# Chunk attention before a squared-ReLU FFN: the first 512 tokens in two halves of the heads, loaded in 1 KB packets

## The chip, the cores and the metric

The kernel runs on one core of a Trainium2 chip. The metric is the device time of one execution in microseconds (us), as the median of several runs. The engines are TensorE (PE, with its weight loads shown apart as PEld), VectorE (DVE), ScalarE (ACT), GpSimd (POOL) and SyncE (SP), which here only issues DMAs.

## What is computed

```python
scores = scale * np.matmul(q_c, k_c.transpose(0, 1, 2, 4, 3))   # chunks of 64 tokens, D = 64
scores = scores - np.max(scores, axis=-1, keepdims=True)
attn = np.exp(scores)
attn = attn / (np.sum(attn, axis=-1, keepdims=True) + 1e-09)
out = np.matmul(attn, v_c)
...
x = np.ascontiguousarray(attn_out.transpose(0, 2, 1, 3)).reshape(B * S, H * D)
h = np.maximum(x @ w_in, 0.0)
return (h * h @ w_out).astype(np.float32)
```

q, k and v are (8, 8, 576, 64): 8 batches, 8 heads, 576 tokens in 9 chunks of 64, 64 numbers a head, all float32. After attention inside each chunk, the 4608 tokens with 512 numbers each go through w_in (512 x 2048), a squared ReLU and w_out (2048 x 512).

## The kernel before

**Tiling.** The tokens are cut into 18 groups of 256 (four chunks each) and the groups into nine blocks of 512. A group's attention makes `x` (token on the partition); its transpose, `xT`, feeds the FFN of the block. `ffn_in` (L359) multiplies by w_in and squares: for each of 16 slices of 128 columns four matmuls (L366), a ReLU on ScalarE (L377) and a square on VectorE (L381) or ScalarE (L379). The second product of block 0 is `ffn_out_by_ft` (L517, matmuls L524), of the later blocks `ffn_out` (L399, matmuls L434), which needs sums of quarters of w_out (`w_sum`, L76) from VectorE.

**Order of the work.** The order is written out by hand. Each engine takes its instructions in the order in which the program names them and waits at semaphores; TensorE too. From L557 to L581 stands the prelude: loads of groups 0 and 1, then their attention, mixed with calls of `keep_busy` (L233), which are matmuls of the identity with itself whose result nobody reads. After it, the loads of the weights are named (L583 to L592), and the loop over blocks (L594) puts the attention of coming groups into numbered slots between the FFN's pieces.

**Loads.** SP issues all loads of one list, one after another: for groups 0 and 1 q, k, q, k (`qk_pieces`, L99: two neighbouring tokens on a partition, all 8 heads, so 512 bytes contiguous in DRAM), then V (`v_pieces`, L145: one token on a partition, 256 bytes contiguous; even heads into `ve_sb`, odd heads into `vo_sb`, the odd ones shifted by 64 partitions, nine DMAs for the two groups), then w_in tile 0, and after it seven more of w_in (`load_w_in`, L159, 1 KB contiguous) and eight of w_out (`load_w_out`, L168). Both weights go through five buffers `w_st` and are cast to bf16 by POOL (L165, L173). A load that finds eight others of the queue unfinished waits for the eighth before it. q and k have five buffers each.

**Attention of a group in the prelude.** `transpose_qk` (L201, as `TE`): 16 transposes on TensorE for q and 16 for k (L190; the high half of each float32 is taken as bf16), copied out of PSUM by VectorE (q) and ScalarE (k), L199. `scores` (L257, as `SC`): 32 matmuls of 64x64 (L276), exp on ScalarE (L287). `values` (L289, as `AV`): for each 128 tokens 16 matmuls (L303) with V, whose extra column of ones gives the sum, then reciprocal (L310) and multiplication (L311) on VectorE. `transpose_x_early` (L218): four transposes (L225) and a copy to `xT` (L230). The FFN of block 0 (`first_ffn_in`, L555) takes its first two slices for tokens 0 to 255, then for tokens 256 to 511, and then the rest for all 512.

**PSUM.** `ps_ffn` has four banks, used in turn by FFN, fillers and these transposes; `ps_att` two double banks.

Of the kernel before, what the change touches and what calls it, by code (L numbers as in the profile page):

```python
# [10 lines left out]
FP32 = mybir.dt.float32  # L11
BF16 = mybir.dt.bfloat16
AF = mybir.ActivationFunctionType
ALU = mybir.AluOpType
# [3 lines left out]
def kernel(  # L18
# [9 lines left out]
    nc = tc.nc  # L28

    B, H, S, D = q.shape  # L30
# [3 lines left out]
    scale = 1.0 / float(D) ** 0.5  # L34
    n_hp = H // 2
    n_dt = d_model // 128
# [4 lines left out]
    blocks = [[g, g + 1] for g in range(0, n_grp, 2)]  # L41
# [6 lines left out]
    chunks = whole[:-2] + rest + whole[-2:]  # L48
# [7 lines left out]
    BT = GT * max(len(b) for b in blocks)  # L56

    const_pool = ctx.enter_context(tc.tile_pool(name="const", bufs=1))
    w_pool = ctx.enter_context(tc.tile_pool(name="w", bufs=1))
    wst_pool = ctx.enter_context(tc.tile_pool(name="wst", bufs=5))  # L60
    in_pool = ctx.enter_context(tc.tile_pool(name="qk", bufs=5))
    att_pool = ctx.enter_context(tc.tile_pool(name="att", bufs=3))
    ffn_pool = ctx.enter_context(tc.tile_pool(name="ffn", bufs=1))
    ps_ffn = ctx.enter_context(tc.tile_pool(name="ps_ffn", bufs=4, space=bass.MemoryType.PSUM))
    ps_att = ctx.enter_context(tc.tile_pool(name="ps_att", bufs=2, space=bass.MemoryType.PSUM))
# [5 lines left out]
    ident = const_pool.tile([128, 128], BF16, name="ident")  # L71
# [4 lines left out]
    w_sum = w_pool.tile([128, 3, n_ft // 2, d_model // 2], BF16, name="w_sum")  # L76
# [22 lines left out]
    def qk_pieces(g):  # L99
        q_sb = in_pool.tile([128, 2, H, D], FP32, name="q_sb")  # L100
        k_sb = in_pool.tile([128, 2, H, D], FP32, name="k_sb")
        qk[g] = (q_sb, k_sb)

        def pairs(dst, src, p, m, b, s):
            return lambda: nc.sync.dma_start(
                out=dst.rearrange("p t h d -> p (t h d)")[p:p + m // 2, :].rearrange(
                    "p (h e) -> p h e", h=H),
                in_=src[b, :, s:s + m, :].rearrange("h (s i) d -> s h (i d)", i=2))

        if is_whole(g):  # L110
            yield pairs(q_sb, q, 0, GT, *chunks[g][0])
        else:
            for c in range(4):
                yield pairs(q_sb, q, c * CH // 2, CH, *chunks[g][c])
        if g < FIRST_DMA_T:
            yield pairs(k_sb, k, 0, GT, *chunks[g][0])
            return
        for t, p, m, b, s in runs(g):
            yield lambda t=t, p=p, m=m, b=b, s=s: nc.sync.dma_start(
                out=k_sb[p:p + m, t, :, :],  # L120
                in_=k[b, :, s:s + m, :].rearrange("h s d -> s h d"))
# [5 lines left out]
    for g in range(n_grp):  # L127
        if is_whole(g):
# [3 lines left out]
            b, s = chunks[g][0]  # L132
# [12 lines left out]
    def v_pieces(g):  # L145
        for t, p, m, b, s in runs(g):
            yield lambda t=t, p=p, m=m, b=b, s=s: nc.sync.dma_start(
                out=v_even[g % NV][p:p + m, t, :, 0:D],
                in_=v[b, 0::2, s:s + m, :].rearrange("h s d -> s h d"))
        for n, p, m, b, s in odd_loads[g]:  # L150
            yield lambda n=n, p=p, m=m, b=b, s=s: nc.sync.dma_start(
                out=v_odd[n % NO][p:p + m, :, 0:D],
                in_=v[b, 1::2, s:s + m, :].rearrange("h s d -> s h d"))

    def go(pieces):
        for f in pieces:
            f()

    def load_w_in(i, n_cast=1):  # L159
        cols = slice(i * 256, (i + 1) * 256)  # L160
        st = wst_pool.tile([128, 1024], FP32, name="w_st").rearrange("p (a f) -> p a f", a=n_dt)
        nc.sync.dma_start(out=st, in_=moe_w_in[:, cols].rearrange("(a p) f -> p a f", p=128))
        n = 256 // n_cast
        for c in range(0, 256, n):
            nc.gpsimd.tensor_copy(  # L165
                out=w_in_bf[:, :, i * 256 + c:i * 256 + c + n], in_=st[:, :, c:c + n])
# [8 lines left out]
    xTs = {}  # L175
    place = {}
# [3 lines left out]
    state = {}  # L180
# [20 lines left out]
    def transpose_qk(g, q_pool, k_pool):  # L201
        if ("qkT", g) not in state:
            state["qkT", g] = att_pool.tile(
                [128, 2, 2, n_hp, 128], BF16, name="qkT", bufs=4)
        qkT = state["qkT", g]
        for which, pool in enumerate((q_pool, k_pool)):
            if pool is None:
                continue
            copy = nc.scalar.copy if which else nc.vector.tensor_copy
            if pool is ps_ffn:  # L210
                bank = pool.tile([128, 512], FP32, name="ps_ffn")
            else:
                bank = pool.tile([128, 1024], FP32, name="ps_att")
            bank = bank.bitcast(BF16)[:, 0:1024]
            transpose_paired(g, which, bank)
            copy_paired(copy, qkT[:, which], bank)

    def transpose_x_early(g, t):  # L218
        j, c = place[g]
        if j not in xTs:  # L220
            xTs[j] = att_pool.tile([128, BT // 128, n_dt, 128], BF16, name="xT", bufs=2)
        psb = ps_ffn.tile([128, 512], FP32, name="ps_ffn").bitcast(BF16)
        x = state["x", g]
        for hp in range(n_hp):
            nc.tensor.transpose(  # L225
                out=psb[:, hp * 128:(hp + 1) * 128],
                in_=x[:, t, hp].rearrange("p a d -> p (a d)"),
                identity=ident)
        copy = nc.vector.tensor_copy if t else nc.scalar.copy
        copy(  # L230
            out=xTs[j][:, c // 128 + t].rearrange("p h q -> p (h q)"), in_=psb[:, 0:512])

    def keep_busy(n):  # L233
        ps = ps_ffn.tile([128, 512], FP32, name="ps_ffn")
        for _ in range(n):
            nc.tensor.matmul(out=ps[:, 0:128], lhsT=ident, rhs=ident, start=True, stop=True)
# [101 lines left out]
    SC, AV, XT = scores, values, transpose_x  # L338
# [4 lines left out]
    def TE(g):  # L343
        transpose_qk(g, ps_ffn, ps_ffn)
# [3 lines left out]

    def TK(g):
        transpose_qk(g, None, ps_ffn)  # L350

    def XE(g):
        for t in range(2):
            transpose_x_early(g, t)

    gTs = {}
    FT_ORDER = [*range(n_ft // 2, n_ft), *range(n_ft // 2)]
# [189 lines left out]
    def pieces(grps):  # L547
        for g in grps:
            yield from qk_pieces(g)
        for g in grps:  # L550
            yield from v_pieces(g)
# [2 lines left out]
    HT = BT // 2  # L554
    first_ffn_in = ffn_in(0, [(0, HT, (0, 1)), (HT, HT, (0, 1)), (0, BT, range(2, n_ft))])  # L555

    go(pieces([0, 1]))  # L557
    load_w_in(0, n_cast=2)
    TE(0)
    keep_busy(8)  # L560
    SC(0)
    keep_busy(6)
    TE(1)
    keep_busy(8)
    SC(1)
    keep_busy(10)
    AV(0, [0])
    keep_busy(4)
    AV(0, [1])
    keep_busy(8)  # L570
    transpose_x_early(0, 0)
    keep_busy(10)
    transpose_x_early(0, 1)
    AV(1, [0])
    keep_busy(8)
    AV(1, [1])
    transpose_x_early(1, 0)
    next(first_ffn_in)
    transpose_x_early(1, 1)
    next(first_ffn_in)  # L580
    keep_busy(4)  # L581

    for i in range(1, 8):  # L583
        load_w_in(i)
# [101 lines left out]
```

## Time and profile before

| what | value |
|---|---|
| runs | 290.56, 291.59, 297.44 us; median 291.59 us |
| profiled execution | span 286.0 us from first to last instruction; its own time is not shown beyond that |
| TensorE busy | 270.7 us, 95% of the span |
| VectorE, ScalarE, GpSimd busy | 187.9, 161.6, 56.5 us |
| DMA | 141841 packets, 57.10 MB |

The profile is one execution recorded by the hardware. Its page gives busy times, a line of 40 equal slices of the span for each engine (a digit is the busy share in tenths), and groups of instructions by line. The timeline lists, in order of time, start, duration, engine, line, operation, output and inputs, and how often; in brackets how long the engine sat idle before it and what released it. The list of waits gives for each engine and line what it waited for: total, times, longest. The DMA view gives packets, bytes and rate in a stretch of time.

### The profile page before, as it was taken

How to read it: one execution, taken by the hardware profiler on the slowest of the kernel's cores; microseconds unless marked ns; L12 is line 12 of the kernel's file. 1: busy time of each engine (PE TensorE's matmuls, PEld its weight loads, DVE VectorE, ACT ScalarE, POOL GpSimd, SP SyncE). 2: the span in 40 equal slices, each digit the busy share in tenths (PEclk: the TensorE clock that was granted, in tenths of full speed). 3: DMA queues.
4: the chain of work that ended last, by engine and by line, in shares of the span. 5: the costliest groups of instructions: out<-in, count | busy, mean ns of one | idle time of the engine just before them, and what ended most of it. 6: DMA issues, size and time to landing. Idle time of an engine off the chain costs nothing. (4 is left out here: it accounts for less than half of the span.)

```text
span 286.0 us, 7260 instructions
## 1 busy us (share of the span) xinstructions
PE 270.7 (95%) x2999; PEld 179.5 (63%) x3002; DVE 187.9 (66%) x307; ACT 161.6 (57%) x272; POOL 56.5 (20%) x89
## 2 busy tenths in 40 slices
PE   1989998999999999999979999999999999999994
PEld 1864444788784488448834784488448844884583
DVE  1274514889872497479637973896479648955792
ACT  1537704687437853885377638763876387318710
POOL 2035933244063002100300021002100300050012
PEclk9999999999999999999999999999999999999999
DMA  7999999999999999999999999399898941232003
GB/s 199 240 320 331 314 330 238 306 215 182 248 233 265 232 223 208 278 252 175 246 224 237 178 201 286 70 154 223 222 254 181 193 154 39 40 92 55 2 18 130
DMA packets 141841, 57.10 MB, mean 200 GB/s; under 512 B 110640, under 2 KB 137520, under 8 KB 141808
## 3 DMA queue, kind: packets, MB, share of 16 engines
q1 hardware_dynamic: 138768, 47.33, 77.1%
q0 software_dynamic: 2896, 9.18, 10.0%
q8 instruction: 23, 0.38, 0.6%
q10 hardware_dynamic: 144, 0.13, 0.1%
q14 instruction: 10, 0.08, 0.1%
HBM read 36.70 MB, written 9.44 MB: 161 GB/s over the span
## 5 line engine op out<-in xcount | busy, mean ns | idle before, releaser
L366 PE MATMUL ps_ffn<-xT,w_in_bf 128*128 128x512 bf16 (+1 forms) x648 | 130.5, 356 | 1.1 <-DVE xT L230 0.7
L381 DVE TENSOR_TENSOR gT<-rl 128x512 bf16<-128x512 f32 (+2 forms) x134 | 75.3, 590 | 63.8 <-ACT rl L377 62.5
L377 ACT ACTIVATE rl<-ps_ffn 128x512 f32<-128x512 f32 (+2 forms) x162 | 86.2, 549 | 28.2 <-PE ps_ffn L366 26.2
L366 PEld LDWEIGHTS <-w_in_bf 128*128 128x128 bf16 x648 | 61.3, 98 | 57.9 <-DVE xT L230 0.9
L434 PEld LDWEIGHTS <-w_st 128*128 128x128 bf16 x640 | 61.9, 98 | 8.2 <-DVE w_st L394 0.9
L394 DVE TENSOR_TENSOR w_st<-gT 128x2048 bf16<-128x2048 bf16 x40 | 47.4, 1219 | 0.2
L434 PE MATMUL ps_ffn<-w_out_bf,w_st 128*128 128x256 bf16 x384 | 45.1, 273 | 0.2
L462 POOL DMA_DIRECT2D out_dram<-o_sb x25 | 17.8, 714 | 128.4 <-DVE o_sb L394 123.8
L434 PE MATMUL ps_ffn<-w_sum,w_st 128*128 128x256 bf16 x256 | 29.6, 273 | 0.0
L434 PEld LDWEIGHTS <-gT 128*128 128x128 bf16 x256 | 24.9, 98 | 4.4 <-DVE gT L381 0.2
L311 DVE TENSOR_TENSOR x<-ps_att,rec 128x512 bf16<-128x512 f32 x36 | 24.9, 692 | 1.2
L514 ACT COPY o_sb<-ps_ffn 128x512 f32<-128x512 f32 (+1 forms) x8 | 4.5, 560 | 35.4 <-PE ps_ffn L434 35.4
L287 ACT ACTIVATE e<-ps_att 128x1024 bf16<-128x1024 f32 x18 | 17.9, 1022 | 7.6 <-PE ps_att L276 7.6
L379 ACT ACTIVATE gT<-rl 128x512 bf16<-128x512 f32 (+2 forms) x28 | 16.8, 599 | 0.9
L434 PE MATMUL ps_ffn<-w_out_bf,gT 128*128 128x256 bf16 x128 | 15.3, 273 | 0.0
L434 PE MATMUL ps_ffn<-w_sum,gT 128*128 128x256 bf16 x128 | 15.3, 273 | 0.0
L524 PE MATMUL ps_ffn<-w_out_bf,gT 128*128 128x512 bf16 x61 | 14.3, 379 | 0.8 <-POOL w_out_bf L173 0.5
L165 POOL CAST w_in_bf<-w_st 128x1024 bf16<-128x1024 f32 (+1 forms) x9 | 9.0, 1002 | 20.2 <-DMA w_st<-in_moe_w_in_dram 20.2
L487 ACT COPY n<-ps_ffn 128x512 f32<-128x512 f32 (+1 forms) x9 | 4.8, 539 | 11.4 <-PE ps_ffn L434 11.4
L303 PEld LDWEIGHTS <-e 64*64 64x64 bf16 x576 | 6.7, 107 | 7.2 <-issue 2.8
L276 PEld LDWEIGHTS <-qkT 64*64 64x64 bf16 x576 | 6.1, 110 | 7.6 <-issue 3.4
L524 PEld LDWEIGHTS <-gT 128*128 128x128 bf16 x64 | 6.0, 98 | 7.7 <-issue 0.8
(52 smaller groups left out, 173.0 us busy)
## 6 DMA issues: line engine op xcount, KB each, us to landing
q_sb<-in_q_dram SPq DMA_DIRECT2D x16, 512.0 KB, 5.8
out_dram<-o_sb POOLq DMA_DIRECT2D x29, 256.0 KB, 4.8
k_sb<-in_k_dram SPq DMA_DIRECT2D x24, 256.0 KB, 5.8
ve_sb<-in_v_dram SPq DMA_DIRECT2D x32, 128.0 KB, 4.3
w_st<-in_moe_w_in_dram SPq DMA_DIRECT2D x8, 512.0 KB, 8.3
w_st<-in_moe_w_out_dram SPq DMA_DIRECT2D x8, 512.0 KB, 6.6
vo_sb<-in_v_dram SPq DMA_DIRECT2D x24, 128.0 KB, 3.7
k_sb<-in_k_dram SPq DMA_DIRECT2D x4, 512.0 KB, 7.5
```

Of the source, the lines that this page charges most:

```text
L165: nc.gpsimd.tensor_copy(out=w_in_bf[:, :, i * 256 + c:i * 256 + c + n], in_=st[:, :, c:c + n])
L287: nc.scalar.activation(out=e_out, in_=s_in, func=AF.Exp, scale=scale)
L303: nc.tensor.matmul(out=ps[64 * p:64 * p + 64, a, hp * (D + 1):(hp + 1) * (D + 1)], lhsT=e[64 * c:64 * c + 64, a, hp, t, :], rhs=vb[64 * c: ...
L311: nc.vector.tensor_tensor(out=x[:, t].rearrange("p h a d -> p a h d"), in0=o[:, :, :, 0:D], in1=rec.to_broadcast([128, 2, n_hp, D]), op=AL ...
L366: nc.tensor.matmul(out=h[:, 0:n], lhsT=w_in_bf[:, dt, ft * 128:(ft + 1) * 128], rhs=xT[:, c // 128:(c + n) // 128, dt, :], start=(dt == 0) ...
L377: nc.scalar.activation(out=rl[:, 0:n], in_=h[:, 0:n], func=AF.Relu)
L379: nc.scalar.activation(out=gT[:, ft, c:c + n], in_=rl[:, 0:n], func=AF.Square)
L381: nc.vector.tensor_tensor(out=gT[:, ft, c:c + n], in0=rl[:, 0:n], in1=rl[:, 0:n], op=ALU.mult)
L394: engine.tensor_tensor(out=out, in0=in0, in1=in1, op=op)
L434: nc.tensor.matmul(out=outs[t], lhsT=a[:, i, t * 128:(t + 1) * 128], rhs=b[:, i, :], start=(first and i == 0 and (last or t == 0)), stop=( ...
L462: dma.dma_start(out=out[t0:t0 + HT, col:col + HD].rearrange("(t p) d -> p t d", p=128), in_=o_sb.rearrange("p (t d) -> p t d", d=HD))
L524: nc.tensor.matmul(out=o_ps[tt], lhsT=gT[:, ft, tt * 128:(tt + 1) * 128], rhs=w_out_bf[:, ft, :], start=(ft == 0), stop=(ft == n_ft - 1))
```

## The change

Only the prelude is changed. The first block's 512 tokens are not taken as two groups of 256 tokens with all heads, but as two halves of the heads (0 to 3, then 4 to 7) with all 512 tokens. `load_half` puts four neighbouring tokens on a partition, so that a head gives 1 KB contiguous, for q, k and V alike: six loads of 512 KB (q, k, V of the first half, then of the second) in place of four and nine. A partition then holds four tokens, and the 64 tokens of a chunk lie on 16 partitions. For q and k the transposes put them in order. For V, which must lie with one token of a chunk on a partition, `spread_v` multiplies by slices of `spread`, a matrix of zeros and ones that POOL makes from the identity: 32 matmuls a half, each with 32 rows (one of four groups of partitions), 128 columns out and 128 columns of V (two heads), summed over the four tokens of a partition into four banks of `ps_ffn`; four copies a half then write V as bf16, with its column of ones, into `v_bf`, which uses memory of `w_sum` before that is needed. Each half gives `x` for four heads of all tokens; `transpose_x_half` writes its part of `xT`. The first two FFN slices of tokens 0 to 255 now come ahead of the last x transpose. The fillers are 24, 4, 6, 4, 4, 4, 6 and 6 (58) in place of 66.

```diff
-    def transpose_x_early(g, t):
...
+    spread = const_pool.tile([128, 240], BF16, name="spread")
+    nc.gpsimd.memset(spread, 0.0)
+    for t in range(4):
+        rows = slice(32 * t, 32 * t + 32)
+        nc.gpsimd.tensor_copy(
+            out=spread[rows, 48:176].rearrange("p (b x) -> p b x", b=2)[:, :, 0:16],
+            in_=ident[rows, 32 * t:32 * t + 32].rearrange("p (b x) -> p b x", b=2))
+        nc.gpsimd.tensor_copy(out=spread[rows, 176:192], in_=ident[rows, 32 * t:32 * t + 16])
+
+    v_bf = w_sum.rearrange("p i f c -> p (i f c)")[:, 0:4 * H * (D + 1)].rearrange(
+        "p (t h d) -> p t h d", t=4, h=H)
+    nc.gpsimd.memset(v_bf[:, :, :, D:D + 1], 1.0)
+
+    def load_half(src, u, name):
+        st = in_pool.tile([128, 2, H, D], FP32, name=name)
+        b, s = chunks[blocks[0][0]][0]
+        nc.sync.dma_start(
+            out=st.rearrange("p t h d -> p (t h d)").rearrange("p (h e) -> p h e", h=4),
+            in_=src[b, 4 * u:4 * u + 4, s:s + BT, :].rearrange("h (s i) d -> s h (i d)", i=4))
...
+    def transpose_half(src, dst, copies):
+        psb = bank_bf16()
+        cols = psb.rearrange("c (h n i p) -> c h i n p", h=2, n=8, i=4)
+        for h in range(2):
+            for i in range(4):
+                for a in range(2):
+                    nc.tensor.transpose(
+                        out=cols[64 * a:64 * a + 64, h, i, :],
+                        in_=src[:, 2 * h + a, i, 1::2],
+                        identity=ident)
+        flat = dst.rearrange("c t h q -> c (t h q)")
+        n = 1024 // len(copies)
+        for i, copy in enumerate(copies):
+            copy(out=flat[:, i * n:(i + 1) * n], in_=psb[:, i * n:(i + 1) * n])
...
+    def scores_half(qkT):
...
+        nc.scalar.activation(
+            out=flat.rearrange("p (b q i) -> p b q i", q=16, i=4),
+            in_=ps.rearrange("p (b i q) -> p b q i", i=4, q=16), func=AF.Exp, scale=scale)
...
+    def spread_v(src, u, copies):
+        outs = [ps_ffn.tile([128, 512], FP32, name="ps_ffn") for _ in range(4)]
+        for a in range(2):
+            for i in range(4):
+                c0 = 48 + 64 * a - 16 * i
+                for t in range(4):
+                    rows = slice(32 * t, 32 * t + 32)
+                    nc.tensor.matmul(
+                        out=outs[t][:, 0:256].rearrange("p (h a d) -> p h a d", h=2, a=2)[:, :, a],
+                        lhsT=spread[rows, c0:c0 + 128],
+                        rhs=src[rows, a::2, i, 1::2],
+                        start=(i == 0), stop=(i == 3))
+        for t, copy in enumerate(copies):
+            copy(
+                out=v_bf[:, t, 4 * u:4 * u + 4, 0:D],
+                in_=outs[t][:, 0:256].rearrange("p (h d) -> p h d", h=4))
...
+    def values_half(e, x, u, j):
...
+    def transpose_x_half(x, u, j, copy):
...
-    go(pieces([0, 1]))
+    A, V = nc.scalar.copy, nc.vector.tensor_copy
+    halves = []
+    for u in range(2):
+        halves.append([load_half(q, u, "q_sb"), load_half(k, u, "k_sb"),
+                       load_half(v, u, ("q_sb", "k_sb")[u])])
     load_w_in(0, n_cast=2)
...
+    keep_busy(24)
+    transpose_half(halves[0][0], qkTs[0][:, 0], [V])
+    keep_busy(4)
+    transpose_half(halves[0][1], qkTs[0][:, 1], [V, A])
     keep_busy(6)
...
+    e0 = scores_half(qkTs[0])
+    spread_v(halves[0][2], 0, [V, V, V, A])
+    transpose_half(halves[1][0], qkTs[1][:, 0], [A])
     keep_busy(4)
...
+    values_half(e0, xs[0], 0, 0)
+    values_half(e0, xs[0], 0, 1)
+    keep_busy(4)
+    transpose_half(halves[1][1], qkTs[1][:, 1], [V, A])
+    transpose_x_half(xs[0], 0, 0, V)
+    transpose_x_half(xs[0], 0, 1, V)
+    keep_busy(4)
+    e1 = scores_half(qkTs[1])
+    spread_v(halves[1][2], 1, [V, V, A, A])
+    keep_busy(6)
+    values_half(e1, xs[1], 1, 0)
+    values_half(e1, xs[1], 1, 1)
+    keep_busy(6)
+    transpose_x_half(xs[1], 1, 0, A)
     next(first_ffn_in)
-    transpose_x_early(1, 1)
     next(first_ffn_in)
-    keep_busy(4)
+    transpose_x_half(xs[1], 1, 1, V)
```

## Prediction

> **What bounds the kernel now.** I read the page first (engine shares, the 40 slices), then who TensorE waited for, then the timeline of the first 24 us, then the DMA view cut at the packet sizes. Two lines of the slices:
>
> ```profile
> PE   1989998999999999999979999999999999999994
> DMA  7999999999999999999999999399898941232003
> ```
>
> TensorE is full in all but the first and last slices, and the DMA engines are full until slice 25 (about 180 us). So two streams run beside each other for most of the kernel, and the change touches only their first 21 us. What TensorE waited for:
>
> ```profile
> PE ps_ffn L190 <- DMA q_sb<-in_q_dram: 5.0, 1, 5.0
> PE ps_att L276 <- DMA qkT<-qkb: 2.6, 3, 1.8
> PE ps_ffn L366 <- DVE xT L230: 0.7, 1, 0.7
> PE ps_ffn L524 <- POOL w_out_bf L173: 0.5, 1, 0.5
> PE ps_att L303 <- DMA vo_sb<-in_v_dram: 0.2, 1, 0.2
> ```
>
> After the prelude these are few: all gaps of TensorE after 21 us add to 4.4 us. Whatever starts the dense part earlier moves the end by as much; a faster DMA stream pays only where a DMA wait stands. The prelude:
>
> ```profile
> 11.16 1.06 PE L190 MATMUL ps_ffn<-ident,k_sb 128*64 128x128 bf16 x16
> 12.15 1.03 PE L236 MATMUL ps_ffn<-ident 128*128 128x128 bf16 x8
> 13.73 0.73 PE L236 MATMUL ps_ffn<-ident 128*128 128x128 bf16 x10
> 17.66 1.17 POOL L165 CAST w_in_bf<-w_st 128x512 bf16<-128x512 f32 x2 [15.47 <-DMA w_st<-in_moe_w_in_dram]
> 18.62 0.60 PE L366 MATMUL ps_ffn<-xT,w_in_bf 128*128 128x256 bf16 x4
> 21.02 9.34 PE L366 MATMUL ps_ffn<-xT,w_in_bf 128*128 128x256 bf16 x45 [0.74 <-DVE xT L230]
> 22.83 1.04 POOL L165 CAST w_in_bf<-w_st 128x1024 bf16<-128x1024 f32 x1 [2.34 <-DMA w_st<-in_moe_w_in_dram]
> ```
>
> The reader is to see three things. The dense part begins at 21.02, when xT of the last 128 tokens is copied; that is the time to beat. The first w_in tile arrives only at 17.66, behind q, k and V, and the eighth (its cast starts at 30.03) follows at about 1.5 us a tile. And TensorE runs at half pace until 13.1: eight fillers take 1.03 us, ten take 0.73 (starts 107 ns, then 56 ns apart), though the granted clock stands at 1.00 throughout.
>
> The DMA view for 4 to 9, 10 to 14 and 15.5 to 25 us, when 512-byte, 256-byte and 1 KB packets move:
>
> ```profile
> DMA packets 2925, 1.47 MB, mean 295 GB/s; under 512 B 47, under 2 KB 2925, under 8 KB 2925
> ...
> DMA packets 3418, 0.86 MB, mean 216 GB/s; under 512 B 3417, under 2 KB 3417, under 8 KB 3417
> ...
> DMA packets 3277, 3.26 MB, mean 344 GB/s; under 512 B 107, under 2 KB 3276, under 8 KB 3276
> ```
>
> **The change part by part.** Loads. Removed: four q and k loads of 512 KB at 512 bytes and nine V loads (1.05 MB) at 256 bytes; added: six loads of 512 KB at 1 KB, the packets of w_in. By the three rates 2.10/295 + 1.05/216 = 7.1 + 4.9 = 12.0 us become 3.15/344 = 9.2 us. SP issues 6 instead of 13 ahead of w_in(0), and no issue waits for the eighth one before it (before, w_in(0) was issued at 12.35, after such waits, and the DMA engines ran nearly dry at 14.3 to 15.0: 56 to 135 GB/s). The first load lands at about 4.9 as now (first transpose 4.99), and each next 1.5 us later: k 6.4, V 7.9, q 9.4, k 10.9, V 12.4. One correction: a 16 KB instruction fetch held one DMA engine for 1.28 us at 12.07, after some 240 TensorE instructions, and the load that crossed it landed late (12.6 to 14.5). The new order reaches that count during the first V matmuls, near 10 us, so I add 1.28: k 12.2, V 13.7. The end of w_in follows at 30.0 - 3.3 = 26.7: 2.8 from the rates, some 0.5 from the dip.
>
> The chain in the new prelude, each step at its row's price (0.05 us from engine to engine). TensorE meets the second k at 12.2: 16 transposes 0.6 (L190 at full pace, as at 42 us; 1.06 at half), qkT copies halved between VectorE and ScalarE, 0.42 and 0.59 (L230, contiguous like the new ones; the old 0.69 is strided): 13.4. The two x transposes and four fillers fit before that. Scores 0.4, to 13.9; exp 1.02 (L287), to 14.9. Beside it TensorE puts V on its partitions, 32 matmuls, to 14.7, and VectorE makes two copies of 128x256 from PSUM, to 15.5. Their price lies between 0.28 (L381, 128x256 from SBUF) and 0.42 (L230); I take 0.35, half of L311's 0.69 at 512 columns; the ends move the result by 0.1 either way. Values 0.3; reciprocal and multiply 0.9 (L310, L311), to 16.8; transposes 0.4; ScalarE's copy 0.59, to 17.9. The first FFN matmul starts at 17.9 against 18.62; w_in(0) (15.2, cast of its first half 0.6) is there. For the other 256 tokens VectorE's xT copy is now behind two squares instead of one: two FFN groups 0.9 with 0.2 of latency, relu 0.39, square 0.28, copy 0.42: 20.2 against 21.02. So the front gives 0.8.
>
> The 64 matmuls that place V are the one new form (32 rows, 128 columns out, four groups of rows into four banks). Bounds: as the score matmuls share the array (32 of 64 columns in 0.43 us at half pace, four at once), 0.45 us for 32; one after another, like the fillers, 1.8 at full and 3.4 at half pace. I take four at once: the scores, also parts of the array with disjoint rows, are the nearest row. One after another gives 22.1; at half pace up to 13.1 as well, 24.5. The pace itself: 24 fillers now run from 1.7 us, so I take full pace from about 8; at half pace to 13.1 the dense part starts at 21.04, a front of 0. Without the fetch it starts at 19.5, a front of 1.5.
>
> What waits behind what: the second k's transposes stand behind both values groups, which wait for exp and the V copies (done 10.1, cover 2 us before k lands); the second q's transposes need the first V copy to free a PSUM bank (9.4, q lands then). POOL gets ten small instructions (0.1 to 0.3 each by its rows at 0.7 to 1.8 us, some 1.5 in all); it is idle from 2.2 to 17.66 now, and the matrices are needed at 8.4. Memory of w_sum holds V until 16; VectorE writes w_sum at 47.7 first. Fillers 66 to 58: nothing on the path.
>
> Behind the front: the 0.14 us wait for w_in(1) at 23.8 goes (its tiles are 3.3 earlier, TensorE 0.8); so does the 0.50 for w_out at 47.2 and the 0.17 for V at 58.1; and the 0.41 for qkT at 75.5, whose transposes stand in SP's queue behind loads. The 1.76 us wait for qkT at 146.5 lies behind the same full queue; of the 3.3 us lead TensorE has used 0.8 + 0.14 + 0.50 + 0.17 + 0.41 = 2.0, so 1.3 would be left, if SP is not tied again to engines by releases of buffers on the way. Between 0 and 1.3 I take half, 0.65. Sum: 0.8 + 0.14 + 0.50 + 0.17 + 0.41 + 0.65 = 2.7 us. The profiled span 286.0 becomes 283.3. The profiled execution's own time is not shown beyond its span; the median of the three runs, 291.59, lies 5.6 above it, so the forecast is 288.9.
>
> Two rules of the Trainium skill speak against this. 512-byte packets moved at 295 GB/s here, 1 KB packets at 344. DMA: Bandwidth & Descriptors, Specifications, sets the least size for full rate at 512 bytes; by that q and k gain nothing, each load keeps 1.78 us and the dense part would start at 21.6; the trace decides. TensorE's pace doubled at 13.1, after a stretch (10.3 to 12.2) that was transposes alone, which speaks for their counting as activity. TensorE: Matmul & The Clock Gate, Part 4, says that transposes do not count as busy for the clock; by it the prelude would stay at half pace, as at the end with 21.04.
>
> **The rivals.** (1) The loads are hidden: the new chain is engine work, and the dense part starts where it did, at half pace (21.04). For: k of the second half lands no earlier than the last k now (10.41). Then only the sure waits go, 0.14 + 0.50 + 0.17 = 0.8: 290.8. (2) The lead is worth all: no fetch in the way (1.5), and the waits go whole, 0.14 + 0.50 + 0.17 + 0.41 + 1.76: 4.5, so 287.1. For: DMA is full up to 160 us, so a lead can last. Against: the fetch hit the last V in the trace. (3) Slower: the V matmuls run one after another and at half pace, start 24.5, 3.5 late; less 0.8 for the waits, 294.3. It decides once the dense part starts later than 21.8. For: no row has four groups of 32 rows; against: the scores do share.
>
> **How the numbers follow.** Likeliest 45%, own range 287.6 to 290.2; rival 1 25%; rival 2 17%; rival 3 10%; 3% left for a new wait later. Two per cent is 5.8 us, about what a measurement of this kernel can tell from no change: faster means under 285.8, slower over 297.4. Rival 2 with its spread passes the first in one case of four, 4%; rival 3 with a new wait the other, 3%. The range leaves out most of rival 3 and the far part of rival 2: 286.3 to 293.0.
>
> **What would show it.** Right: 1 KB loads landing 1.5 us apart; 32 V matmuls in under 0.8 us; first FFN matmul near 17.9, the dense part near 20.2; no wait of L524's for w_out; the w_in casts ending near 28. Wrong: a dense part after 21; V matmuls 50 ns or more apart; qkT waits that grow; a second k later than 12.2.

## The result, and the profile after

| kernel | median us (lowest to highest, runs) | profiled execution: time, span |
|---|---|---|
| before | 292.77 (286.19 to 297.44, 20) | span 286.0 |
| after | 293.35 (290.02 to 296.88, 20) | 295.69, span 293.9 |

The ratio of after to before is 1.0119 [1.0074, 1.0163]; it leaves disturbed runs out, while the medians are over all runs. The change made the kernel about 1% slower, or did nothing: the means of all runs differ by 1.2 us [-0.4, 2.8]. (Here and below, figures in square brackets are 95% intervals.) The forecast gain of 2.7 us is excluded either way.

Around the span lie 1.8 us in after, and 1.7 to 1.9 in every other profiled kernel below, not the 5.6 that the forecast used. So the profiled execution of before took about 286.0 + 1.8 = 287.8 us, five less than its median: it was a lucky one.

The slices of after:

```profile
PE   7769999999999999899869999999999769999994
PEclk9999999999999999999999999999999959999999
DMA  7999999979999999999999999789699942133003
```

TensorE is fuller in the first slice than before, less so in slices 2 and 3, and has dents at slices 20 and 21 (140 to 154 us) and 32 and 33 (228 to 243). In the second dent the granted clock is low. What TensorE waited for (total, times, longest):

```profile
PE ps_att L374 <- DMA qkT<-qkb: 7.5, 5, 2.4
...
PE ps_att L269 <- issue: 1.2, 1, 1.2
PE ps_ffn L460 <- DMA xT<-x: 1.0, 1, 1.0
...
PE ps_ffn L460 <- DVE xT L327: 0.7, 1, 0.7
```

The wait for transposed q and k is 7.5 us where before had 2.6. Its largest parts, in the timeline:

```profile
149.54 0.45 PE L374 MATMUL ps_att<-qkT 64*64 64x64 bf16 x32 [2.39 <-DMA qkT<-qkb]
...
236.52 0.64 PE L374 MATMUL ps_att<-qkT 64*64 64x64 bf16 x32 [2.17 <-DMA qkT<-qkb]
238.35 0.64 PE L374 MATMUL ps_att<-qkT 64*64 64x64 bf16 x32 [1.19 <-DMA qkT<-qkb]
```

The first stands where before waited 1.76 us; of the other two, one stands where before waited 0.40 us, and one is new. The same 32 matmuls take 0.64 us instead of 0.45 there, at the lower clock. The prelude of after on TensorE:

```profile
8.70 0.64 PE L288 MATMUL ps_ffn<-q_sb,spread 32*128 32x128 bf16 x32
...
13.58 0.28 PE L269 MATMUL ps_att<-qkT 64*64 64x64 bf16 x9
15.02 0.38 PE L269 MATMUL ps_att<-qkT 64*64 64x64 bf16 x23 [1.17 <-issue]
15.34 0.64 PE L288 MATMUL ps_ffn<-k_sb,spread 32*128 32x128 bf16 x32
...
18.51 0.38 PE L460 MATMUL ps_ffn<-xT,w_in_bf 128*128 128x256 bf16 x2
...
21.29 1.03 PE L460 MATMUL ps_ffn<-xT,w_in_bf 128*128 128x256 bf16 x7 [0.69 <-DVE xT L327]
```

The 32 placing matmuls take 0.64 us, so they do run several at once. Then TensorE stops for 1.17 us in the middle of the second scores, after nine of 32, and waits for nothing that the profile shows ("issue"). Without the stop the dense part would start at about 20.1 (an estimate, 21.29 - 1.17); it starts at 21.29. The DMA view for the windows 4 to 9, 9 to 14 and 15.5 to 25 us of after:

```profile
DMA packets 1683, 1.67 MB, mean 334 GB/s; under 512 B 51, under 2 KB 1683, under 8 KB 1683
...
DMA packets 1790, 1.80 MB, mean 359 GB/s; under 512 B 50, under 2 KB 1789, under 8 KB 1789
...
DMA packets 3086, 3.37 MB, mean 355 GB/s; under 512 B 107, under 2 KB 2800, under 8 KB 3084
```

The loads did what was forecast: 334 and 359 GB/s where the old ones had 295 and 216; w_in's first tile is cast from 14.17 (17.66 before), its last lands at 25.30. By the bytes that SP's queue had moved, after leads at 30 us by 9.8 to 8.2 MB, at 60 by 17.0 to 15.7. At 90 us the lead is gone, 22.0 to 21.9, which fits loads that wait for buffers that the engines free. At 148 us after is behind, 32.3 to 32.5.

### The profile page after: what moved, and what is told of

Its sections match the earlier page's. It is cut to its first block, busy times and chain, and to the rows that moved or that the text cites. A ratio compares the mean times of both kernels' runs of the same rounds, so it can differ in the third digit from the quotient of the medians.

```text
span 293.9 us, 7385 instructions
## 1 busy us (share of the span) xinstructions
PE 273.6 (93%) x3058; PEld 180.9 (62%) x3058; DVE 189.8 (65%) x312; ACT 162.8 (55%) x273; POOL 57.4 (20%) x99
## 5 line engine op out<-in xcount | busy, mean ns | idle before, releaser
L460 PE MATMUL ps_ffn<-xT,w_in_bf 128*128 128x512 bf16 (+1 forms) x648 | 132.4, 360 | 2.4 <-DMA xT<-x 1.0
L460 PEld LDWEIGHTS <-w_in_bf 128*128 128x128 bf16 x648 | 62.0, 99 | 60.6 <-issue 5.4
L488 DVE TENSOR_TENSOR w_st<-gT 128x2048 bf16<-128x2048 bf16 x40 | 48.1, 1239 | 0.2
L556 POOL DMA_DIRECT2D out_dram<-o_sb x25 | 17.8, 714 | 132.2 <-DVE o_sb L488 127.1
L528 PEld LDWEIGHTS <-gT 128*128 128x128 bf16 x256 | 24.9, 98 | 4.3 <-DVE gT L475 0.2
L409 DVE TENSOR_TENSOR x<-ps_att,rec 128x512 bf16<-128x512 f32 x32 | 22.1, 691 | 1.1
L385 ACT ACTIVATE e<-ps_att 128x1024 bf16<-128x1024 f32 x16 | 16.1, 1021 | 10.8 <-PE ps_att L374 10.8
L374 PE MATMUL ps_att<-qkT 64*64 64x64 bf16 x512 | 7.2, 201 | 7.5 <-DMA qkT<-qkb 7.5
L551 POOL DMA_DIRECT2D out_dram<-o_sb x8 | 4.8, 606 | 30.7 <-DVE o_sb L488 30.4
```

The costliest lines, as they stand in the source:

```text
L374: nc.tensor.matmul(out=ps[64 * c:64 * c + 64, o0:o0 + 64], lhsT=qkT[64 * a:64 * a + 64, 1, t, hp, cols], rhs=queries(a, t, hp, p), start=T ...
L385: nc.scalar.activation(out=e_out, in_=s_in, func=AF.Exp, scale=scale)
L409: nc.vector.tensor_tensor(out=x[:, t].rearrange("p h a d -> p a h d"), in0=o[:, :, :, 0:D], in1=rec.to_broadcast([128, 2, n_hp, D]), op=AL ...
L460: nc.tensor.matmul(out=h[:, 0:n], lhsT=w_in_bf[:, dt, ft * 128:(ft + 1) * 128], rhs=xT[:, c // 128:(c + n) // 128, dt, :], start=(dt == 0) ...
L488: engine.tensor_tensor(out=out, in0=in0, in1=in1, op=op)
L528: nc.tensor.matmul(out=outs[t], lhsT=a[:, i, t * 128:(t + 1) * 128], rhs=b[:, i, :], start=(first and i == 0 and (last or t == 0)), stop=( ...
```

## The experiments

The theories at the start. A: the front came, but the stop, a half clock that its gaps bring, and a late wait with a fixed end eat it. B: the spread of the runs is as large as the change, and my base was lucky. A third was formed only when the runs on the late waits had shaken A. C: something else in the new prelude slows the later blocks. Kernels whose name begins with b are the kernel before with an edit, the others the changed kernel with one, c_before apart. Medians are of all runs of a kernel, beside those of before in the same call.

### The same two kernels again

Edit: none.

> The kernel before once more, unchanged: how much does one execution differ from the next? Theory L (late waits): the prelude repeats within 0.3 us (dense part at 21.0), but the waits of TensorE for qkT after 110 us do not; they add to more than the 2.2 us of the first profile (0.41 + 1.76), up to 8, and where they are long the granted clock falls to half for some us. Rival N (no such noise): the gaps after 40 us are those of the first profile within 0.5 us, span 285.5 to 286.5. Ratio to the kernel before 0.995 to 1.005 by both.

> The changed kernel once more, unchanged. Theory F (instruction fetch): the 1.17 us stop in the second half's scores repeats within 0.2 us at the same matmul, dense part at 21.2 to 21.4. Theory L: TensorE is 1.4 to 2.0 us ahead of the kernel before at its scores near 72 us, and the waits for qkT after 110 us take that away, by another sum than the 7 us of the first profile. Rival S (systematic): the same waits at the same places within 0.5 us (0.8 at 120, 3.4 at 146, 3.4 at 235). Ratio 1.00 to 1.016.

Measured: before again 292.67 us (12 runs) beside 293.95, ratio 1.0092 [1.0009, 1.0175]; after again 294.24 (6), 1.0194 [1.0086, 1.0303]. A kernel against itself came out 0.9% off by the ratio (by the means of all runs 0.1 us faster [-2.5, 2.7]), so B holds for differences under one per cent. In c_before the waits for w_out (0.5) and V (0.17) are absent, and the late wait for q and k is 2.12 us instead of 1.76: the waits that the forecast called sure belonged to one execution. All its waits for transposing DMAs come to 7.3 us, where the first profile had 2.6:

```profile
PE ps_att L276 <- DMA qkT<-qkb: 5.0, 4, 2.1
...
PE ps_ffn L366 <- DMA xT<-x: 2.3, 1, 2.3
```

In c_after the stop is there again, at the same place (1.20 us after nine of 32 second scores); half clock held from 17.1 for 6.8 us.

### Where the stop comes from

e_wide makes the fillers four times as wide and a quarter as many:

```diff
-            nc.tensor.matmul(out=ps[:, 0:128], lhsT=ident, rhs=ident, start=True, stop=True)
+            nc.tensor.matmul(out=ps[:, 0:w], lhsT=ident, rhs=wide[:, 0:w], start=True, stop=True)
```

> The fillers become four times wider and a quarter as many (58 matmuls of 128 columns become 16 of up to 512), so TensorE has 84 fewer instructions in the prelude. Theory F: the stop of TensorE is at instruction 449 of its stream, so it leaves the scores of the second half and stands in the middle of the second V placing (about its 13th of 32 matmuls), 0.5 to 2 us long; dense part 20.5 to 22. Rival W: the stop is a wait of these scores for something that the profile does not show; then it stays at the tenth score matmul, 1.2 us, dense part 21.3. If neither, the stop is gone and the dense part starts at 20.1. Time within 0.7% of the changed kernel's by all.

e_early puts 40 tiny matmuls into the prelude in place of eight fillers:

```diff
-    keep_busy(24)
+    keep_busy(16)
+    tiny = ps_att.tile([128, 1024], FP32, name="ps_att")
+    for _ in range(40):
+        nc.tensor.matmul(
+            out=tiny[0:32, 0:8], lhsT=ident[:, 0:32], rhs=ident[:, 0:8], start=True, stop=True)
```

> The changed kernel with 16 fillers and 40 tiny matmuls (8 columns) in place of the first 24 fillers: 64 TensorE instructions more, all in the time before q lands. Theory F (place): the stop stands at instruction 449 again, which now is some 64 instructions earlier, at the x transposes of the first half or the last k transposes, near 12.3 us. What sets its end is open: if the fetch is asked for when TensorE reaches a count, it comes 1 us or more earlier and the dense part starts at 20.3 to 20.8; if it only waits its turn behind loads handed to the DMA engine before, the fetch runs at 12.0 to 12.8 as in all four kernels so far, the stop ends near 15 and is 2 us or longer, and the dense part starts at 21.0 to 21.6. The time moves by less than 0.7% by both.

Measured: e_wide 294.19 us (6 runs; before 293.95), ratio 1.0212 [1.012, 1.0303]; e_early 299.23 (6; before 291.42), 1.02 [1.0093, 1.0306]. The stop of e_wide, then that of e_early, in their timelines:

```profile
13.93 0.35 PE L288 MATMUL ps_ffn<-k_sb,spread 32*128 32x128 bf16 x11
14.98 0.52 PE L288 MATMUL ps_ffn<-k_sb,spread 32*128 32x128 bf16 x21 [0.70 <-issue]
```

```profile
17.42 0.34 PE L334 MATMUL ps_ffn<-ident 128*128 128x128 bf16 x3
19.74 0.34 PE L334 MATMUL ps_ffn<-ident 128*128 128x128 bf16 x3 [1.98 <-issue]
```

With fewer instructions ahead the stop moved from the scores into the placing of V; with more of them it moved into fillers. Counted as instructions of TensorE it stands at 446 in after and c_after, 445 in e_wide, 702 in e_early, and 702 is 446 + 256. An instruction fetch is 16 KB in the trace. That places the stop by instruction count, not by operation or data. In all these runs the stop ends 1.3 to 1.6 us after such a fetch is over (after: fetch from 12.59 to 13.71, stop until 15.02), so TensorE had most likely outrun its instructions; the trace does not say for which engine a fetch is. Before fetched from 12.07 to 13.35 and reached the 446th only at about 16.96 us, without a stop. For e_early the stop had been expected at that count again, near 12.3 us; e_early passed it without one. The tiny matmuls also left TensorE at half pace until 13.9 us, against 7.75 in after.

### Packets of 512 bytes

```diff
-        nc.sync.dma_start(
...
+        for y in range(2):
+            nc.sync.dma_start(out=dst[:, :, y, :], in_=rows[:, :, y, :])
```

> The changed kernel with each of its six loads cut into two DMAs of 512-byte packets; all else as changed. By the step on loads the halves land 1.8 us apart instead of 1.5, the second k near 12.1, V near 13.9, w_in at the end 1.5 to 2 us later than with 1 KB. Theory F with the queue: the instruction fetch waits behind packets already handed to a DMA engine, smaller ones go faster, so the stop of 1.17 us shrinks below 0.5; dense part 20.5 to 21.5. Rival: the fetch does not care for packet size, the stop stays at 1.0 or more and the dense part starts at 22 or later. Ratio to the kernel before 1.00 to 1.015 by both.

Measured: 300.06 us (6 runs; before 293.95), 1.0393 [1.0295, 1.0491]. Second k landed at 12.38 (11.14 in after), second V at 15.27 (12.65), the last of w_in at 27.49 (25.30); dense part at 21.61. So in the prelude 512-byte packets cost 1.2 us by the second k and 2.6 by the second V, the size of packet that the change is about; but the stop shrank to 0.29 and the dense part lost only 0.3. The other six microseconds came later, in waits for transposed q and k (9.0 us in sum) and in half clock (13.7 us, where after has 6.8), and the front doesn't explain them.

### The half clock

b_thin takes 34 fillers out of the prelude of before, from the values on; e_fill is e_wide with more fillers in the gaps:

```diff
     AV(0, [0])
-    keep_busy(4)
     AV(0, [1])
-    keep_busy(8)
...
```

> The kernel before without its fillers after the first value group (34 of its 66 matmuls): TensorE then idles some 2.5 us more between 14.7 and 21 us. It doubles the suspected cost in the kernel that does not have it. Theory C: the clock is lost in the first FFN, a half-speed stretch of 3.4 or 6.8 us begins at 15 to 24 us, mean clock of the runs 0.983 or lower against 0.989, median 1.5 to 3.5 us above the kernel before's. Rival L: no half-speed stretch ahead of 110 us, mean clock 0.987 to 0.991, median within 1 us of the kernel before's. The dense part starts at 20.8 to 21.3 by both.

> The changed kernel with wide fillers (a quarter as many, as before) and more of them in the gaps of the second half: 8 columns-of-128 more between the two x transposes, 20 instead of 6 after the V placing (in a bank that is free, so they do not wait for the V copies), 16 instead of 6 ahead of the last x transposes, 8 and 12 more around the first FFN groups. Theory C (clock): the changed prelude leaves TensorE idle 4.0 to 4.8 us where the kernel before leaves 1.6 to 2.0, and this drops the granted clock to half for 3.4 or 6.8 us in most executions; with the gaps filled the mean granted clock of the runs rises from 0.983 to 0.989 or more, no half-speed stretch begins before 30 us, and the median falls by 1.5 us or more against the changed kernel's, to 291 to 292.5. Rival L (late waits alone): the clock falls only behind the late waits for qkT, mean clock stays 0.982 to 0.985, median 293 to 294.5. The dense part starts at 21.2 to 21.8 by both.

Measured: b_thin 295.65 us (6 runs; before 291.42), 1.02 [1.0136, 1.0263]; e_fill 293.69 (6), 1.0107 [1.0037, 1.0176]. The clock of b_thin:

```profile
PEclk9979999999999999999959999999999979999999
```

Its third slice shows it: after gaps of 0.4 to 1.0 us in the prelude the granted clock falls to half for 3.4 us from 18.4, though TensorE was busy for 9.1 of the 12 us up to 16. In e_fill it does not fall in the first 30 us. That supports the theory of the clock for the prelude, but not every execution shows it (after's own kept full clock through its stop of 1.17 us), and e_fill was not faster than before.

### The late waits

b_late moves the casts and transposing DMAs of coming q and k to earlier slots in before; the kernels with late3 in their name also move scores, values and x (a_late3 in after, f_late3 in e_fill, g_late3 in f_late3 with 48 small first fillers).

```diff
-            slots = {SC: (4, 4), AV: (7, 11), XT: (10, 14), C: (18, 22), TD: (20, 24)}
+            slots = {SC: (4, 4), AV: (7, 11), XT: (10, 14), C: (15, 18), TD: (17, 20)}
```

> The kernel before with the casts and DMA transposes of q and k of the coming blocks named three to four slots earlier (C at 15 and 18, TD at 17 and 20 instead of 18, 22 and 20, 24; blocks 1 and 2 keep their own slots). Theory L: the waits for qkT from 170 us on (0.4 in the first profile, 2.6 in the second) come from transposes issued too late; with about 3 us more lead those behind 150 us fall below 0.5 in sum, the clock stays full more often (mean 0.991 or more), and the median falls 1.5 to 3 us below the kernel before's. Rival Q (queue): the transposes stand behind the same loads in SP's queue and land no earlier, or the casts push ScalarE's ReLUs; median within 1 us.

> The kernel before with later use and earlier making of qkT in blocks 2 to 8: scores two to three slots later (7, in block 3 at 11, for the shared groups 10), values and x transposes with them, casts at 15 and 18, DMA transposes at 17 and 20. Theory L: a slot is about 0.87 us, so each transpose has 5 to 6 us more; the waits for qkT behind 110 us, 2.2 to 6 us in sum so far, fall below 1 us, the clock keeps full pace (mean 0.996 or more) and the median lies 3 to 5 us below the kernel before's, runs spread less than 5 us. Rival Q: the transposes are late because the DMA queue is, and whatever is asked for earlier lands as late; median 0 to 2 us below.

> The changed kernel with the same later use and earlier making of qkT as b_late3. It tells what the change is worth once the late waits no longer take it. Theory A (absorbed): the change's front, 0.3 us late to 0.9 us early at the second block, shows at the end: a_late3 within 1 us of b_late3, if the clock in the prelude holds; where it is lost (half-speed stretch before 30 us in about half of the executions) 1.7 to 3.4 us slower, so its median 0.5 to 2.5 us above b_late3's. Rival T (the change itself disturbs the later stream): 3 us or more above b_late3, with late waits that remain.

> a_late3 with the wide and additional fillers of e_fill. Theories A and C: no half-speed stretch in the prelude, the stop for instructions 0.7 us at instruction 445; block 1 starts at 51.0 to 51.6, as in the undisturbed executions of the kernel before, and the median is within 0.7 us of b_late3's and 0.5 to 2 us below a_late3's. Rival T: 2 us or more above b_late3.

> f_late3 with 48 small fillers (64x64) in place of the first six wide ones: the same busy time ahead of the first transposes, 84 TensorE instructions more. Theory F: instruction 446 now stands near the x transposes of the first half (about 12.3 us), and its fetch is asked for some 2 us earlier, as in e_early, so there is no stop of over 0.3 us in the prelude (702 is reached in the FFN, by when the second fetch is there); dense part at 20.2 to 20.7, the time that the prediction had, and the median 0.3 to 1.2 us below f_late3's. If the fetch is not earlier: a stop of 2 us near 12.3, dense part after 21.2. Against b_late3: 0.5 us faster to 0.5 us slower by theory A.

| kernel | median us (runs) | before | ratio |
|---|---|---|---|
| b_late | 289.21 (6) | 291.42 | 0.9809 [0.9712, 0.9906] |
| b_late3 | 290.31 (12) | 294.62 | 0.9963 [0.9903, 1.0023] |
| a_late3 | 297.54 (6) | 294.62 | 1.0251 [1.0164, 1.0339] |
| f_late3 | 297.06 (12) | 294.62 | 1.0123 [0.9971, 1.0274] |
| g_late3 | 298.44 (6) | 294.62 | 1.0261 [1.0103, 1.0418] |

The late waits have a price in before: by the means of all runs b_late3 is 4.0 us faster than before [2.0, 6.0], and its wait for transposed q and k is 0.4 us (one of 2.6 for x is left). b_late alone does not show it: its ratio rests on two of its six runs, by the means of all it is 2.7 us faster [-1.9, 7.3], and its profile still waits 4.4 us. But the slots of b_late3 behind the new prelude gave 297 to 298 us against 290, even in g_late3, whose prelude has no stop and no half clock and whose second block starts at 50.8 us (52.6 in before, 51.2 in c_before). One wait of a_late3 is enough to see it:

```profile
239.18 2.31 PE L460 MATMUL ps_ffn<-xT,w_in_bf 128*128 128x512 bf16 x5 [7.83 <-DMA xT<-x]
```

The transposing DMA of that xT landed 6.4 us after its issue, that of the same block in b_late3 after 3.4. The instructions are the same there. Theory A has no place for this; so theory C was formed.

### What in the new prelude reaches the later blocks

Four kernels on one chip. g_fill is e_fill with the 48 small first fillers (no stop, no half clock in the prelude); g_late is g_fill with b_late's slots, a_late is after with them. b_spread is the kernel before with only the table that the change adds, read by nobody:

```diff
+    spread = const_pool.tile([128, 240], BF16, name="spread")
+    nc.gpsimd.memset(spread, 0.0)
```

> Edit: the changed kernel with its 24 first fillers replaced by 48 small ones (64x64 outputs), the later fillers four times as wide, and more of them in the gaps of the prelude; the slots of the later attention as in the kernel before. In an earlier kernel with this prelude no stop of TensorE appeared in the prelude and the clock held there. Theory 'stop and clock' (what the new front gains is eaten by the stop of 1.2 us and by the half clock, nothing else): the front gain of about 1 us comes out at the end, ratio to the kernel before about 0.993 to 0.997, that is 1 to 2 us below it. Theory 'absorbed' (the wait for the transposed q and k of the fourth block ends at the same time whatever comes earlier, so what is gained ahead of it is waited away there): ratio 1.00 within 0.005, with that wait grown by about the front gain. Theory 'something else of the new prelude harms later blocks': ratio above 1.01.

> Edit: the kernel g_fill with the casts and transposing DMAs of the coming groups' q and k moved from slots 18, 22 and 20, 24 to 15, 18 and 17, 20, as it was done to the kernel before (there it gave a ratio of 0.981). Theories 'stop and clock' and 'absorbed': the wait for transposed q and k goes, and with it the absorption, so the time is that of the kernel before with these slots, or 1 us less: ratio 0.975 to 0.985 to the kernel before. Theory 'something else of the new prelude harms later blocks': above 1.00.

> Edit: the changed kernel itself with the same move of the casts and transposing DMAs (15, 18 and 17, 20). Theory 'absorbed': the late waits go as they did in the kernel before, the stop and the half clock of the prelude stay, ratio to the kernel before about 0.985 to 0.995. Theory 'something else of the new prelude harms later blocks': the move gives less than 1 us here, ratio 1.00 or more.

> Edit: the kernel before with the table of 480 bytes a partition that the change adds, filled with zeros by GpSimd and read by nobody, so that all later tiles lie 480 bytes further on in SBUF, as in the changed kernel. Theory 'addresses': the later waits and transfers become slower as in the changed kernel, ratio 1.01 or more. All others: ratio 1.00 within 0.007.

| kernel | median us (runs) | before | ratio |
|---|---|---|---|
| g_fill | 297.61 (4) | 293.25 | 1.0146 [1.0064, 1.0228] |
| g_late | 294.66 (10) | 293.25 | none given; by the means of all runs 2.7 us slower [0.4, 5.1] |
| a_late | 294.14 (10) | 293.25 | 1.0183 [1.0105, 1.0261] |
| b_spread | 301.47 (4) | 293.25 | 1.0263 [1.0194, 1.0331] |

A falls: with stop and half clock taken from the prelude, g_fill is no faster, and b_late's slots, though they make g_late 2.3 us faster than g_fill [0.2, 4.4], leave it 2.7 us slower than before. And a table of 480 bytes a partition that nobody reads costs the old kernel about 8 us. In b_spread's waits and DMA issues:

```profile
PE ps_att L279 <- DMA qkT<-qkb: 10.1, 5, 3.7
...
PE ps_ffn L369 <- DMA xT<-x: 3.0, 1, 3.0
```

```profile
qkT<-qkb SPq DMA_TRANSPOSE x14, 7.2
```

The same issue line of before:

```profile
qkT<-qkb SPq DMA_TRANSPOSE x14, 6.0
```

The prelude of b_spread is as before's (second block at 51.8 us); the loss is in waits for the transposing DMAs, 13 us where before had 2.6 and c_before 7.3, and in half clock (10.2 us, none in before and c_before ahead of their last microseconds). The median from issue to landing is 7.2 us, not 6.0, and 13 of the 14 transposing DMAs of q and k take longer than the same one in before. The engines' own work does not: the ReLU of 512 columns to float32 takes 595 to 596 ns after 60 us in before, b_spread and a_pad (described below). The table moves every later tile by 480 bytes. The sources of those DMAs (`qkb`), the staged output, gT and rl start at multiples of 512 bytes in before, as the program lays them out; in b_spread, as in after, they start 32 bytes short of one.

### Only the addresses

a_pad is the changed kernel with the table declared 512 bytes wide; g_late_pad is g_late with it (and wide fillers fed from repeated columns of the identity, to make room).

```diff
-    spread = const_pool.tile([128, 240], BF16, name="spread")
+    spread = const_pool.tile([128, 256], BF16, name="spread")
```

> Edit: the changed kernel with its table of zeros and ones declared 512 bytes a partition (256 columns) instead of 480; the last 16 columns are zeros and are never read. Only addresses change: in the kernel before, the transposing DMAs' sources and targets and the gated hidden tiles start at multiples of 64 bytes; in the changed kernel all of them start 32 bytes off such a multiple; with 512 bytes they are at multiples of 64 again. Theory 'addresses' (the table of 480 bytes alone cost the kernel before about 8 us, ratio 1.026): most of that comes back, ratio to the kernel before 0.980 to 0.995, and the wait for transposed q and k in the fourth block shrinks under 2 us. Theory 'the memset or its place, not the addresses, slowed the kernel with the table': no change from the changed kernel, ratio 1.00 to 1.02.

> Edit: g_late (no stop and no half clock in the prelude, casts and transposing DMAs of the coming groups in slots 15, 18 and 17, 20) with the table declared 512 bytes a partition, and the wide fillers fed by repeating columns of the identity instead of a table of their own, for space. Theory 'addresses': the kernel before gained a ratio of 0.981 by these slots, and the front gives up to 1 us more, so 0.970 to 0.982, the best of all kernels here. Rival: 0.995 to 1.01, as g_late.

Measured: a_pad 290.04 us (287.62 to 292.25, 12 runs) beside 293.57 for before, ratio 0.9949 [0.9904, 0.9995]; g_late_pad 288.68 (12), 0.9825 [0.9759, 0.9892]. By the means of all runs a_pad is 4.2 us faster than after and c_after together [3.0, 5.3], in other calls, c_after on another chip; g_late_pad is 6.7 faster than g_late [4.5, 8.8], both on one chip. Against before in their own calls, after is 1.2 us slower and a_pad 3.7 us faster [2.2, 5.3]. a_pad has the memset and the table too, so neither of them is what slowed b_spread. Waits of a_pad, the scores of its fourth block, and its slices:

```profile
PE ps_att L374 <- DMA qkT<-qkb: 2.4, 1, 2.4
...
PE ps_att L269 <- issue: 1.5, 1, 1.5
```

```profile
148.96 0.71 PE L374 MATMUL ps_att<-qkT 64*64 64x64 bf16 x64
```

```profile
PEclk9956999999999999999999999999999999999999
```

The wait for transposed q and k is back from 7.5 to 2.4 us, and none of it stands in the fourth block, where 64 score matmuls run in one piece. That is so though the stop of TensorE (1.5) and the half clock of the prelude (10.2 us of it) are still there and the dense part of this execution starts only at 22.86. In g_late_pad both are gone as well:

```profile
PE   7799999999999999999999999999999889999994
PEclk9999999999999999999999999999999999999998
```

It is the fastest of these kernels that keeps the new prelude; from b_late, the old prelude with the same slots, the runs do not tell it apart (0.5 us less by the means [-5.0, 4.0]).

All profiled executions together, worked out from the traces: gaps of TensorE over 0.3 us after 30 us, half clock between 8 and 278 us, and the time that 99 in 100 packets of 256 bytes on SP's queue stay under, after 30 us.

| kernels | late gaps us | half clock us | 256-byte packets, 99th of 100 |
|---|---|---|---|
| seven at the old addresses or padded to 512 | 2.8 to 8.7, mean 5.2 | mean 4.4 | 44 to 52 ns |
| thirteen shifted by 480 bytes (six of them, with the table of the wide fillers, by 1504) | 5.1 to 13.0, mean 9.3 | mean 8.7 | 51 to 92 ns |

The median packet is 18 ns in all 20. 4.1 us of gaps and 4.3 us at half clock (some 2.1 lost) give about 6 us, between the 4.2 of after and the 8 of b_spread. The two groups differ in slots and fillers too, so this is a sum of the right size and no proof; that the addresses cost the time is shown by b_spread and a_pad. The way from the address to the wait is argued, not shown: that the shift lengthens the tail of the packets, that this makes the transposing DMAs late, and that the longer waits bring more half clock. From one execution to the next, tail and gaps do not go together (a_late3 has 51 ns and 12.7 us, f_late3 59 ns and 5.1 us).

Not settled: which of the DMAs (transposes, V, stores) is slowed by which address, and whether the step that counts is 64 bytes, 256 or another; the runs tried shifts of 480, 512 and 1504 only (480 and 1504 leave the same remainder of 512). Before with a padded table was not run, so how much of the gain of a_pad and g_late_pad over before is the new prelude, and how much the move by 512 bytes, stays open too. The Trainium skill, DMA: Bandwidth & Descriptors, How a descriptor splits into AXI transactions, says that a transaction must start at a 256-byte boundary, so that a descriptor which starts off one costs beats for bytes that are not used. The trace agrees in the direction, in the tail alone: were every packet of 256 bytes split in two, the median of 18 ns could be expected to move, and it did not.

## Why the prediction was wrong

**The step that failed.** The forecast costed the table by what makes it ("POOL gets ten small instructions") and found it hidden. That it lies in SBUF ahead of nearly all other tiles, and moves them by 480 bytes, was given no price, and neither the forecast nor any of its rivals named it; only the 3% for a new wait later leave room for it. It is worth 4.2 us in this kernel (after against a_pad) and decides the sign: with the padded table the same change measures 290.04 us beside 293.57 for before. That this is near the forecast of 288.9 and its gain of 2.7 is luck: the dense part of a_pad starts at 22.86, so no front is in it. Two of the forecast's own signs of being wrong came: a dense part after 21, and waits for transposed q and k that grow.

**Right: the loads, and by luck the end of the chain.** Loads 1.5 us apart; second k 11.14 (12.2 forecast), second V 12.65 (13.7), w_in's last tile 25.30 (26.7); the placing of V 0.64 us for 32 (under 0.8); full pace from 7.75 us (about 8). The chain would have ended at about 20.1 (20.2), but two errors cancel there: the second k came 1.06 us early, and the steps behind it took 1.0 us longer, because VectorE was still busy (its half of the copy of k started at 12.89) and ScalarE's half waited for VectorE's (13.33), where the forecast had them side by side and done at 13.4:

```profile
12.89 0.41 DVE L256 COPY qkT<-ps_ffn 128x512 bf16<-128x512 bf16 x1
...
13.33 0.58 ACT L256 COPY qkT<-ps_ffn 128x512 bf16<-128x512 bf16 x1 [1.72 <-DVE qkT L256]
```

**Wrong: the fetch.** It was priced as a delay of one load, 1.28 us. The loads were not late. The same 16 KB read struck as a stop of TensorE, 1.17 us, once TensorE ran ahead of it: the dense part at 21.29, a front of nothing instead of 0.8. Rival 1 has nearly that number (21.04), for another reason: half pace, which ended at 7.75. The forecast gives its ends of 21.04, 22.1 and 24.5 without the steps to them.

**Wrong: the sure waits.** 0.14, 0.50 and 0.17 us were read from one execution, and a second one of the same kernel has not the last two. The lead of 3.3 us in the loads, from which the 0.65 at 146.5 us was to come, was given back by 90 us; there TensorE waited 0.99 and 2.39 us instead of 1.76.

**Wrong: the base.** The sum stood on an execution of some 287.8 us as if it were the median. Its small late waits (2.6 us for q and k, 5.0 in c_before) left less to gain and hid what the kernel is sensitive to: transposing DMAs that land just in time.

**Missing: the clock.** That gaps in the prelude cost the clock (6.8 us at half in c_after, 10.2 in a_pad, none in before) was foreseen for the first microseconds only, not for what follows a stop. It is not so each time: after's own profile has the stop and no half clock in the prelude.

## What to carry to other kernels

A new tile moves the addresses of all tiles behind it: look at the start addresses of what DMAs read and write before and after an edit, and pad the new tile so that they keep their remainders, here with 512 bytes instead of 480. Before a forecast leans on small waits, see them in a second execution, and compare the profiled execution's own time with the median. If a prelude packs more instructions into the first microseconds, count them against the instruction fetches as well as against the engines.

## What the runs showed of the hardware

- Moving all later tiles by 480 bytes made this DMA-heavy kernel 2.6% slower [1.9, 3.3], with no other work added than one memset. The changed kernel, with the memset in it, was 4.2 us faster [3.0, 5.3] when the move was 512 bytes.
- TensorE stopped for 0.3 to 2.0 us at its 445th, 446th or 702nd instruction, whichever operation that was, until 1.3 to 1.6 us after a 16 KB instruction fetch was over; before came to its 446th at 16.96 us, 3.6 us after the fetch, and did not stop.
- The granted clock fell to half in stretches of 3.4, 6.8 or 10.2 us, after gaps from 0.4 us up, in the prelude as well as at the late waits; in after's prelude a gap of 1.17 us did not bring it.
- 32 matmuls of 32 rows in four groups of rows took 0.64 us, where 32 fillers one after another take 1.8 at full pace (32 starts of 56 ns).
